# Cross attention into a silu MLP on one core: the opening reordered, softmax sums in halves, x loads moved

## The chip, the cores and the metric

The kernel runs on one core of one Trainium2 chip. The metric is the device time of one execution in microseconds (us); lower is better. Before the change the median of five runs is 222.99 us (222.26 to 225.28).

## The reference

For each of 8 batches and 8 heads there are 512 tokens `x` and 32 states `state` of width 64. Tokens read from states and states read from tokens; the results are joined along the sequence, the heads are merged, and 4352 rows of width 512 go through a two-layer MLP with silu (2048 wide).

```python
scores = scale * np.matmul(x, state.transpose(0, 1, 3, 2))
a = softmax(scores); xread = np.matmul(a, state)        # 512 rows of a batch
scores2 = scale * np.matmul(state, x.transpose(0, 1, 3, 2))
a2 = softmax(scores2); sread = np.matmul(a2, x)         # 32 rows of a batch
...
h = x @ w_in                                            # 512 -> 2048
return (h / (1 + exp(-h))) @ w_out                      # 2048 -> 512
```

## The kernel before

All products are in bf16 with fp32 sums. The kernel never builds `xread`: with `W1[b] = state[b] @ w_in` (line 248, from the transposed states `sbd`), the first MLP layer of a batch's 512 tokens is `W1[b]` times the transposed probabilities `aT`. For a batch b the names are:

- `x_f` holds x in fp32, two buffers by b % 2. `x_n` is x in bf16 (with columns of ones for the softmax sums), `x_u` the same in another order, `xT` its transpose. Batches 0 and 1 are cast by `cast_x` and transposed on PE (`x_T`, evicted by `x_Te`); batches 2 to 7 are cast by `cast_xu` and transposed by a DMA on the SP queue (`x_Td`).
- `sc` makes the scores (PE), `ex` their exponentials `en` (ACT), `norm_s` the row sums and reciprocals `rs` (DVE), `norm_m` the probabilities `an` (DVE or POOL). `a_T` (PE) or `a_Td` (a DMA on the SP queue, batches 3 to 7) transposes them to `aT`. `sread_m`, `sread_n`, `sread_t` make the 32 state rows.
- `g1(b, ft)` is one of 16 blocks of the first layer, two matmuls of 512 columns and a silu on ACT; `g2` is one matmul of the second layer, 64 to a batch. `G2(b, ft)` is four of them. The 256 state rows of all batches are batch 8.
- `w1_m` and `w1_e` compute and evict one quarter j of `W1`; `W1x` is both. Quarter j needs the load `load_wi(j)`, and `g2` of ft 4j to 4j+3 needs `load_wo(j)`. These loads are issued by POOL, one after the other, and turn fp32 into bf16 on the way.
- `warm(n, bank, w)` issues n matmuls of zeros that nobody reads.

The order of each engine's queue is written out by hand (`tc.manual_schedule`): each engine takes its instructions in program order. The program has an opening (lines 328 to 411), a hand-laid mixture of batches 0 and 1 (413 to 486), and then `phase(k, fill)` for k = 1 to 7: 64 `g2` of batch k are numbered as steps, and `fill` hangs the attention and the 16 `g1` of batch k + 1 on given steps. `att_head` places the transposing load `x_Td` and the scores of a batch, `att_tail` its softmax, `W1`, `a_Td` and `g1`.

In the opening of the kernel before, POOL issues `load_wi(0)`, `load_wo(0)`, `load_st(1)`, `load_wi(1)` as soon as the states of batch 0 are cast; only batch 0 goes through attention; x of batch 1 is loaded by POOL between weight loads, and batch 1's casts, transposes, scores and softmax lie between the `g1` and `G2` of batch 0. In phase k, `load_x(k+2)` is issued on SP at the phase's start, `cast_xu(k+2)` follows on POOL in the same phase, and `a_Td(k+1)` is issued on SP a few us later.

Of the kernel before, what the change touches and what calls it, by code (L numbers as in the profile page):

```python
# [8 lines left out]
FP32 = mybir.dt.float32  # L9
# [10 lines left out]
def kernel(  # L20
# [8 lines left out]
    nc = tc.nc  # L29
# [10 lines left out]

    zeros = pers.tile([128, 512], BF16, name="zeros")
    ident = pers.tile([128, 128], BF16, name="ident")
    st0_f = pers.tile([128, 128], FP32, name="st0_f")
    st_nat = pers.tile([128, B, 128], BF16, name="st_nat")
    sbd = pers.tile([128, B, KT, 2, NS], BF16, name="sbd")
    x_f = [pers.tile([128, KT, 2, 256], FP32, name=f"x_f{i}") for i in range(2)]
# [30 lines left out]
    def cp(eng, dst, src):  # L77
        if eng == "dve":
            nc.vector.tensor_copy(dst, src)  # L79
        elif eng == "pool":  # L80
            nc.gpsimd.tensor_copy(dst, src)  # L81
        else:
            nc.scalar.activation(dst, src, func=COPY, bias=0.0)  # L83
# [5 lines left out]
    def load_x(b, eng, kt=0, n=4):  # L89
        dst = x_f[b % 2][:, ds(kt, n)].rearrange("p k h e -> p (k h) e")  # L90
        eng.dma_start(dst, x_src(b, kt, n))  # L91
# [4 lines left out]
    def load_wi(j):  # L96
        nc.gpsimd.dma_start(
            w_in_sb[:, :, ds(512 * j, 512)], win_re[:, :, ds(512 * j, 512)]
        )

    def load_wo(j):
        nc.gpsimd.dma_start(w_out_sb[:, ds(4 * j, 4), :], wout_re[:, ds(4 * j, 4), :])

    def load_st(b):
        nc.gpsimd.dma_start(st_nat[:, b, :], state[b].rearrange("h ns d -> ns h d"))


    def cast_x(b, eng, kts=(0, 1, 2, 3)):
        for kt in kts:
            for h in range(2):  # L110
                cp(
                    eng,
                    x_n[b % 2][:, kt, :, ds(2 + D * h, D)],
                    x_f[b % 2][:, kt, h, :].rearrange("p (c d) -> p c d", c=4),
                )
# [11 lines left out]
    def x_T(b, kt, bk):  # L127
        v = bf(bk).rearrange("p (k c t) -> p k c t", k=2, c=4)
        for c in range(4):
            nc.tensor.transpose(  # L130
                v[:, kt % 2, c, :], x_n[b % 2][:, kt, c, ds(2, 128)], ident[:]
            )

    def x_Te(b, kt, n, bk, eng):
        v = bf(bk).rearrange("p (k c t) -> p k c t", k=2, c=4)
        cp(eng, xT[b % 2][:, ds(kt, n)], v[:, ds(kt % 2, n)])
# [32 lines left out]
    def ex(b, kt, n, bk):  # L169
        v = bank[bk][:].rearrange("p (k q s) -> p k q s", k=2, q=8)  # L170
        nc.scalar.activation(  # L171
            en[b % 2][:, :, :, ds(kt, n), :].rearrange("p h c k s -> p k (h c) s"),
            v[:, ds(kt % 2, n)],
            func=EXP,
            bias=0.0,
            scale=SCALE,
        )
# [83 lines left out]
    def w1_e(b, j, bks, engs):  # L261
        for half in range(2):
            cp(engs[half], W1[b % 2][:, half, ds(512 * j, 512)], bank[bks[half]][:])
# [55 lines left out]
    def warm(n, bk, w=128):  # L319
        for i in range(n):  # L320
            nc.tensor.matmul(  # L321
                bank[bk][:, 0:w], zeros[:, 0:128], zeros[:, 0:w], start=True, stop=True,
                skip_group_check=True,
            )

    with tc.manual_schedule():

        nc.scalar.dma_start(st0_f[:], state[0].rearrange("h ns d -> ns h d"))
        for kt in range(KT):
            load_x(0, nc.sync, kt, 1)  # L330
        nc.vector.memset(zeros[:], 0.0)  # L331
        nc.vector.memset(sbd[:], 0.0)
        for i in range(2):
            nc.vector.memset(x_n[i][:, :, :, 1:131:129], 1.0)
        make_identity(nc, ident[:])
        nc.scalar.preload_act_table(EXP)
        cp("pool", st_nat[:, 0, :], st0_f[:])
        load_wi(0)
        load_wo(0)
        load_st(1)  # L340
        load_wi(1)
        warm(30, "o0")

        XB = ("o0", "o1", "w0", "w1")
# [13 lines left out]
            w1_e(b, j, bks, engs)  # L358

        def exs(b):  # L360
            ex(b, 0, 2, "a0")
            ex(b, 2, 2, "a1")

        def xTs(b, q, eng):
            for kt in (2 * q, 2 * q + 1):
                x_T(b, kt, AB[q])
            x_Te(b, 2 * q, 2, AB[q], eng)

        def scs(b, q):
            for kt in (2 * q, 2 * q + 1):  # L370
# [1 line left out]


        cast_x(0, "dve", (0,))
        x_T(0, 0, XB[0])
        x_Te(0, 0, 1, XB[0], "act")
        cast_x(0, "dve", (1,))
        st_T(0, "a1", "act", "dve")
        cast_x(0, "dve", (2, 3))
        warm(8, "w1")  # L380
        x_T(0, 1, XB[1])
        x_Te(0, 1, 1, XB[1], "act")
        sc(0, 0, SB[0])
        ex(0, 0, 1, SB[0])
        warm(10, "w1")
        x_T(0, 2, XB[2])
        x_Te(0, 2, 1, XB[2], "act")
        sc(0, 1, SB[1])
        ex(0, 1, 1, SB[1])
        warm(5, "o0")  # L390
        x_T(0, 3, XB[3])
        x_Te(0, 3, 1, XB[3], "dve")
        warm(4, "o0")
        for kt in (2, 3):
            sc(0, kt, SB[kt])
            ex(0, kt, 1, SB[kt])
        norm_s(0, 0, 2)
        norm_m(0, "pool", 0, 2)
        norm_s(0, 2, 2)
        norm_m(0, "dve", 2, 2)  # L400
        nc.scalar.preload_act_table(SILU)
        warm(8, "o0", 512)
        w1_m(0, 0, ("w0", "w1"))
        w1_e(0, 0, ("w0", "w1"), ("act", "act"))
        a_T(0, (("a0", "dve"), ("a1", "dve")))
        warm(2, "o0", 512)
        load_x(1, nc.gpsimd, 0, 2)
        load_x(1, nc.gpsimd, 2, 2)
        load_wo(1)
        load_wi(2)  # L410


        for ft in range(4):
            g1(0, ft)
        G2(0, 0)
        st_T(1, "a0", "dve", "dve")
        sread_m(0, "a1")
        sread_n(0, "a1")
        G2(0, 1)
        sread_t(0, "a1", "dve")  # L420
        G2(0, 2)
        W1x(0, 1, AB, DA)
        G2(0, 3)
        g1(0, 4)
        cast_x(1, "dve", (0, 1))
        cast_x(1, "pool", (3,))
        g1(0, 5)
        W1x(1, 0, AB, DA)
        g1(0, 6)
        cast_x(1, "dve", (2,))  # L430
        load_wo(2)
        load_wi(3)
        load_wo(3)
        load_x(2, nc.gpsimd)
        for b in range(2, B):
            load_st(b)
        g1(0, 7)
        xTs(1, 0, "dve")
        xTs(1, 1, "act")
        G2(0, 4)  # L440
        scs(1, 0)
        scs(1, 1)
        exs(1)
        nc.scalar.preload_act_table(SILU)
        G2(0, 5)
        W1x(0, 2, HB, DD)
        norm_s(1)
        norm_m(1, "dve")
        G2(0, 6)
        g1(0, 8)  # L450
        G2(0, 7)
        g1(0, 9)

        W1x(1, 1, AB, ("act", "act"))
        g1(0, 10)
        G2(0, 8)
        g1(0, 11)
        a_T(1, (("a0", "dve"),))
        G2(0, 9)
        g1(1, 0)  # L460
        W1x(1, 2, AB, DA)
        G2(0, 10)
        g1(1, 1)
        W1x(0, 3, AB, DA)
        G2(0, 11)
        g1(0, 12)
        g1(0, 13)
        W1x(1, 3, AB, DA)
        cast_xu(2, "dve", (0, 1))
        cast_xu(2, "pool", (2, 3))  # L470
        x_Td(2)

        G2(0, 12)
        g1(0, 14)
        G2(0, 13)
        g1(0, 15)
        g1(1, 2)
        G2(0, 14)
        st_T(2, "a0", "dve", "dve")
        g1(1, 3)  # L480
        G2(0, 15)
        g1(1, 4)
        g1(1, 5)
        for tt in range(4):
            o_e(0, tt, OB[tt], "dve")
        load_x(3, nc.sync)


        WP = (("w0", "w1"), ("h0", "h1"))
# [22 lines left out]
        def att_head(fill, b, s0, s1):  # L512
            add(fill, s0, L(st_T, b, "a0", "dve", "dve"))
            add(fill, s0, L(x_Td, b))
            add(fill, s1, L(scs, b, 0))
            add(fill, s1 + 2, L(scs, b, 1))

        def att_tail(fill, b, s, a0, sg, dg):
            add(fill, s, L(exs, b), L(W1p, b, 0), L(norm_s, b))
            add(fill, s, L(norm_m, b, "dve", 0, 2), L(norm_m, b, "pool", 2, 2))  # L520
            add(fill, s, L(nc.scalar.preload_act_table, SILU))
            add(fill, s + 14, L(W1p, b, 1), L(sread_m, b, "a1"), L(sread_n, b, "a1"))
            if b == 2:
                add(fill, a0, L(a_T, b, (("a0", "act"),)))
            else:
                add(fill, s, L(a_Td, b))
            add(fill, a0 + 2, L(sread_t, b, "a1", "dve"))
            for i in range(16):
                add(fill, sg + dg * i, L(g1, b, i))

        fill = {}
        for i in range(6, 16):
            add(fill, i - 6, L(g1, 1, i))
        add(fill, 1, L(sread_m, 1, "a1"), L(sread_n, 1, "a1"))
        add(fill, 3, L(sread_t, 1, "a1", "dve"))
        add(fill, 3, L(cast_xu, 3))
        add(fill, 6, L(scs, 2, 0))
        add(fill, 8, L(scs, 2, 1))
        att_tail(fill, 2, 10, 33, 38, 1.55)
        att_head(fill, 3, 37, 58)  # L540
        phase(1, fill)

        for k in range(2, 7):
            fill = {}
            if k + 2 < B:
                load_x(k + 2, nc.sync)
            att_tail(fill, k + 1, 0, 24, 35, 1.8)
            if k + 2 < B:
                add(fill, 0, L(cast_xu, k + 2))
                att_head(fill, k + 2, 34, 56)  # L550
            phase(k, fill)
# [45 lines left out]
```

The softmax here doesn't subtract the row's maximum and nothing guards it: scores larger than these inputs give would overflow.

## Time and profile before

| | us |
|---|---|
| median of five runs | 222.99 (222.26 to 225.28) |
| the profiled execution, its own time | 222.26 |
| its span, first to last instruction | 220.5 |
| PE busy (with 67 warm matmuls of zeros) | 212.9 |
| ACT, DVE, POOL busy | 133.0, 83.6, 40.7 |
| TensorE clock granted | 1.000 |

Two tables of the page give the weights of the groups. A busy PE matmul of 512 columns has a duration of 379 ns, but such matmuls follow each other every 216 ns, because they overlap; sums over PE are therefore made from the starts. In the timeline a line reads: start, length, engine, line, operation, output<-input, shape and count, and in brackets how long the engine idled before it and for whom. Lines of `cp` (79, 81, 83) serve many casts and evictions, so they are told apart by their tiles.

### The profile page before, as it was taken

The page shows a single profiled execution, that of the slowest core. Times are in us where ns is not written, and L with a number is a line of the kernel's source. Part 1 is how long each engine was busy: PE and PEld are TensorE (multiplying, and loading weights), DVE is VectorE, ACT ScalarE, POOL GpSimd, SP SyncE. Part 2 cuts the span into 40 slices and gives each one's busy share as a digit, 9 for nine tenths or more (in the row PEclk, how much of TensorE's full clock was granted, in tenths as well). Part 3 has the DMA queues.
Part 4 walks back from the last instruction along what each step waited for, and adds up shares of the span by engine and source line. Part 5 has one row for each costly group of instructions (what it writes and reads, how often), then busy time and mean ns, then how long its engine had stood idle before and what let it go on. Part 6 is the DMA issues. An engine that isn't in the chain of part 4 may idle for free.

```text
span 220.5 us, 4100 instructions
## 1 busy us (share of the span) xinstructions
PE 212.9 (97%) x1659; PEld 103.6 (47%) x1659; DVE 83.6 (38%) x162; ACT 133.0 (60%) x219; POOL 40.7 (18%) x78
## 2 busy tenths in 40 slices
PE   7999999999999999999999999997999999999993
PEld 7644443443445344444444444443453444566552
DVE  4736445614910671048213831285105701111110
ACT  3755966579587927684577647781769377533210
POOL 4643822005200060005200250025000200000000
PEclk9999999999999999999999999999999999999999
DMA  6999998892251576138611763075511311111112
GB/s 199 152 246 244 171 250 132 123 292 68 95 109 37 123 210 146 48 84 230 166 48 50 218 167 92 3 231 154 95 48 48 98 48 49 50 49 48 48 51 95
DMA packets 36068, 26.52 MB, mean 120 GB/s; under 512 B 20816, under 2 KB 31312, under 8 KB 36048
## 3 DMA queue, kind: packets, MB, share of 16 engines
q1 hardware_dynamic: 28800, 19.27, 32.3%
q0 software_dynamic: 6688, 6.52, 16.5%
q10 hardware_dynamic: 560, 0.46, 0.6%
q8 instruction: 13, 0.21, 0.4%
q14 instruction: 7, 0.06, 0.1%
HBM read 17.30 MB, written 8.91 MB: 119 GB/s over the span
## 4 chain that ended last, share of the span: by engine, by line
PE 84%; DMA 8%; POOL 2%; ACT 2%; issue 2%; DVE 1%; ACTq 0%; POOLq 0%; DVEq 0%
PE ps_o L296 45%; PE ps_h L272 24%; DMA w_in_sb<-in_moe_w_in_dram 6%; PE ps_h L283 3%; PE ps_w L296 3%; DMA aT<-an 2%; PE ps_o L321 2%; PE ps_h L251 2%; PE ps_w L251 2%; PE ps_a L160 1%; POOL an L186 1%; PE ps_a L218 1%; POOL x_f L91 1%; PE ps_w L321 1%; PE ps_a L251 1%
## 5 line engine op out<-in xcount | busy, mean ns | idle before, releaser
L296 PE MATMUL ps_o<-w_out_sb,g 128*128 128x512 bf16 x480 | 129.5, 379 | 0.0
L280 ACT ACTIVATE g<-ps_h 128x512 bf16<-128x512 f32 x128 | 75.7, 597 | 53.7 <-PE ps_h L272 52.1
L272 PE MATMUL ps_h<-aT,W 128*128 128x512 bf16 x256 | 75.4, 379 | 1.9 <-DMA aT<-an 1.4
L296 PEld LDWEIGHTS <-g 128*128 128x128 bf16 x512 | 47.6, 98 | 51.7 <-issue 2.8
L79 DVE COPY o_sb<-ps_o 128x512 f32<-128x512 f32 x30 | 20.6, 688 | 89.8 <-PE ps_o L296 89.7
L272 PEld LDWEIGHTS <-W 128*128 128x128 bf16 x256 | 24.5, 98 | 32.3 <-issue 1.7
L186 POOL TENSOR_TENSOR an<-en,rs 128x512 bf16<-128x512 bf16 x7 | 10.0, 1425 | 91.7 <-ACT W L83 52.1
L81 POOL CAST x_u<-x_f 128x256 bf16<-128x256 f32 x44 | 15.6, 404 | 26.5 <-DMA x_f<-in_x_dram 24.8
L79 DVE CAST W<-ps_w 128x512 bf16<-128x512 f32 x24 | 15.3, 680 | 4.5 <-PE ps_w L251 4.5
L83 ACT ACTIVATE W<-ps_h 128x512 bf16<-128x512 f32 x24 | 13.1, 602 | 0.1
L291 ACT ACTIVATE g_s<-ps_h 128x256 bf16<-128x256 f32 x16 | 6.1, 384 | 11.1 <-PE ps_h L283 11.1
L181 DVE TENSOR_REDUCE rs<-en 128x32 f32<-128x1024 bf16 (+1 forms) x9 | 9.9, 1099 | 5.9 <-ACT en L171 5.9
L283 PE MATMUL ps_h<-xsT,w_in_sb 128*128 128x256 bf16 x64 | 9.6, 273 | 0.0
L296 PE MATMUL ps_w<-w_out_sb,g 128*128 128x512 bf16 x32 | 9.5, 379 | 0.0
L171 ACT ACT_TABLE_LOAD x7 | 9.0, 1283 | 0.1
L171 ACT ACTIVATE en<-ps_a 128x512 bf16<-128x512 f32 (+1 forms) x16 | 8.4, 568 | 0.2
L283 PEld LDWEIGHTS <-w_in_sb 128*128 128x128 bf16 x64 | 6.3, 98 | 4.1
L251 PEld LDWEIGHTS <-sbd 64*32 64x32 bf16 x256 | 3.2, 89 | 10.1 <-issue 10.0
L321 PE MATMUL ps_o<-zeros 128*128 128x128 bf16 (+1 forms) x49 | 6.7, 309 | 1.2 <-DVE zeros L331 1.2
L510 ACT ACT_TABLE_LOAD x6 | 7.7, 1283 | 0.1
L160 PEld LDWEIGHTS <-xT 128*128 128x128 bf16 x128 | 5.9, 98 | 3.5 <-DVE xT L79 0.3
L321 PEld LDWEIGHTS <-zeros 128*128 128x128 bf16 x67 | 6.0, 127 | 1.9 <-DVE zeros L331 1.2
(63 smaller groups left out, 124.9 us busy)
## 6 DMA issues: line engine op xcount, KB each, us to landing
out_dram<-o_sb SPq DMA_DIRECT2D x32, 256.0 KB, 2.4
x_f<-in_x_dram SPq DMA_DIRECT2D x5, 1024.0 KB, 6.9
w_in_sb<-in_moe_w_in_dram POOLq DMA_DIRECT2D x4, 512.0 KB, 9.4
w_out_sb<-in_moe_w_out_dram POOLq DMA_DIRECT2D x4, 512.0 KB, 9.1
x_f<-in_x_dram SPq DMA_DIRECT2D x4, 256.0 KB, 3.7
x_f<-in_x_dram POOLq DMA_DIRECT2D x2, 512.0 KB, 8.5
x_f<-in_x_dram POOLq DMA_DIRECT2D x1, 1024.0 KB, 13.5
out_dram<-o_sb ACTq DMA_DIRECT2D x1, 256.0 KB, 2.4
```

The source lines that it names most:

```text
L79: nc.vector.tensor_copy(dst, src)
L81: nc.gpsimd.tensor_copy(dst, src)
L83: nc.scalar.activation(dst, src, func=COPY, bias=0.0)
L171: nc.scalar.activation(en[b % 2][:, :, :, ds(kt, n), :].rearrange("p h c k s -> p k (h c) s"), v[:, ds(kt % 2, n)], func=EXP, bias=0.0, sc ...
L181: nc.vector.tensor_reduce(v, en[b % 2][:, :, :, ds(kt, n), :], axis=AX, op=ADD)
L186: e.tensor_tensor(an[b % 2][:, :, :, ds(kt, n), :].rearrange("p h c k s -> p (h c) k s"), en[b % 2][:, :, :, ds(kt, n), :].rearrange("p h ...
L251: nc.tensor.matmul(bank[bks[half]][ds(32 * kt, 32), :], sbd[ds(64 * half, 64), b, kt, half, :], w_in_sb[ds(64 * half, 64), kt, ds(512 * j, ...
L272: nc.tensor.matmul(bk[:], W1[b % 2][:, half, ds(128 * ft, 128)], aT[b % 2][:, half, :, :], start=(half == 0), stop=(half == 1), skip_group ...
L280: nc.scalar.activation(g[b % 2][:, ft, :], bk[:], func=SILU, bias=0.0)
L283: nc.tensor.matmul(bk[:, 0:256], w_in_sb[:, kt, ds(128 * ft, 128)], xsT[:, kt, :, :, :], start=(kt == 0), stop=(kt == KT - 1), skip_group_ ...
L296: nc.tensor.matmul(bank[bk][:, c0:c1], src[:, ft, ds(128 * tt, 128)], w_out_sb[:, ft, c0:c1], start=(ft == 0), stop=(ft == 15), skip_group ...
L321: nc.tensor.matmul(bank[bk][:, 0:w], zeros[:, 0:128], zeros[:, 0:w], start=True, stop=True, skip_group_check=True,)
```

## The change

- States of batch 1 get an fp32 buffer of their own (`st_f[1]`), loaded by SP. All of x of batch 1 is loaded by SP directly behind x of batch 0, in four pieces.
- Casts of batches 0 and 1 are split over DVE, POOL and ACT (`cast_x` takes a list of heads). `load_wi(0)` and `load_wo(0)` stand on POOL behind four casts, the last of them of batch 1's first piece; the other weight loads stand behind POOL's two products of batch 0's softmax, and the last two behind its product of batch 1's.
- Batch 1's casts, transposes, scores and exponentials are done in the opening, ahead of the first `W1x(0, 0)`; one pair of activation table loads goes. The mixture of batches 0 and 1 is laid anew: ten `g1` of batch 1 instead of six stand in it.
- `att_tail` forms the softmax sums and products of a batch in two halves, the first product on POOL, the second on DVE.
- `load_x` of batches 4 to 7 moves one phase ahead: it is issued behind `x_Td` in `att_head`, or at step 6 of phase 1 (batch 4). Phase 1 places batch 2's attention 4 steps earlier.

```diff
+        for kt in range(KT):
+            if kt == 2:
+                nc.sync.dma_start(st_f[1][:], state[1].rearrange("h ns d -> ns h d"))
+            load_x(1, nc.sync, kt, 1)
...
-        cp("pool", st_nat[:, 0, :], st0_f[:])
-        load_wi(0)
-        load_wo(0)
-        load_st(1)
-        load_wi(1)
...
+        cp("pool", st_nat[:, 0, :], st_f[0][:])
         x_T(0, 0, XB[0])
         x_Te(0, 0, 1, XB[0], "act")
         cast_x(0, "dve", (1,))
         st_T(0, "a1", "act", "dve")
-        cast_x(0, "dve", (2, 3))
+        cast_x(0, "dve", (2,), (0,))
+        cast_x(0, "pool", (2,), (1,))
+        cast_x(0, "dve", (3,), (0,))
+        cast_x(0, "pool", (3,), (1,))
+        cast_x(1, "pool", (0,), (1,))
+        load_wi(0)
+        load_wo(0)
...
         x_T(0, 3, XB[3])
+        cast_x(1, "dve", (0,), (0,))
         x_Te(0, 3, 1, XB[3], "dve")
...
+        cast_x(1, "dve", (1,))
+        cast_x(1, "act", (2,))
         norm_s(0, 0, 2)
         norm_m(0, "pool", 0, 2)
+        x_T(1, 0, "o0")
+        x_T(1, 1, "o0")
+        x_Te(1, 0, 2, "o0", "dve")
+        cp("act", st_nat[:, 1, :], st_f[1][:])
+        cast_x(1, "act", (3,))
+        warm(8, "a0")
+        st_T(1, "a1", "dve", "dve")
         norm_s(0, 2, 2)
-        norm_m(0, "dve", 2, 2)
+        norm_m(0, "pool", 2, 2)
+        x_T(1, 2, "o1")
+        x_T(1, 3, "o1")
+        x_Te(1, 2, 2, "o1", "act")
+        warm(4, "a0")
+        sc(1, 0, "w0")
+        sc(1, 1, "w0")
+        ex(1, 0, 2, "w0")
+        warm(8, "a0")
+        sc(1, 2, "w1")
+        sc(1, 3, "w1")
+        ex(1, 2, 2, "w1")
         nc.scalar.preload_act_table(SILU)
-        warm(8, "o0", 512)
-        w1_m(0, 0, ("w0", "w1"))
-        w1_e(0, 0, ("w0", "w1"), ("act", "act"))
+        warm(8, "a0")
         a_T(0, (("a0", "dve"), ("a1", "dve")))
-        warm(2, "o0", 512)
-        load_x(1, nc.gpsimd, 0, 2)
-        load_x(1, nc.gpsimd, 2, 2)
+        W1x(0, 0, ("o0", "o1"), DA)
+        load_wi(1)
         load_wo(1)
         load_wi(2)
+        load_wo(2)
+        norm_s(1, 0, 2)
+        norm_m(1, "pool", 0, 2)
+        norm_s(1, 2, 2)
+        norm_m(1, "dve", 2, 2)
+        warm(6, "o0")
...
+        for j in (1, 2, 3):
+            n = 3 * j - 3
+            g1(0, 4 * j)
+            g1(1, n)
+            W1x(1, j, AB, DA)
...
         def att_head(fill, b, s0, s1):
             add(fill, s0, L(st_T, b, "a0", "dve", "dve"))
             add(fill, s0, L(x_Td, b))
+            if 4 < b + 1 < B:
+                add(fill, s0, L(load_x, b + 1, nc.sync))
...
         def att_tail(fill, b, s, a0, sg, dg):
-            add(fill, s, L(exs, b), L(W1p, b, 0), L(norm_s, b))
-            add(fill, s, L(norm_m, b, "dve", 0, 2), L(norm_m, b, "pool", 2, 2))
+            add(fill, s, L(exs, b), L(W1p, b, 0))
+            add(fill, s, L(norm_s, b, 0, 2), L(norm_m, b, "pool", 0, 2))
+            add(fill, s, L(norm_s, b, 2, 2), L(norm_m, b, "dve", 2, 2))
...
-        for i in range(6, 16):
-            add(fill, i - 6, L(g1, 1, i))
-        add(fill, 1, L(sread_m, 1, "a1"), L(sread_n, 1, "a1"))
-        add(fill, 3, L(sread_t, 1, "a1", "dve"))
-        add(fill, 3, L(cast_xu, 3))
-        add(fill, 6, L(scs, 2, 0))
-        add(fill, 8, L(scs, 2, 1))
-        att_tail(fill, 2, 10, 33, 38, 1.55)
+        for i in range(10, 16):
+            add(fill, i - 10, L(g1, 1, i))
+        add(fill, 2, L(scs, 2, 0))
+        add(fill, 3, L(scs, 2, 1))
+        att_tail(fill, 2, 6, 30, 35, 1.8)
+        add(fill, 6, L(cast_xu, 3), L(load_x, 4, nc.sync))
...
-            if k + 2 < B:
-                load_x(k + 2, nc.sync)
```

More of the change, by code (lines that the diff above doesn't have):

```diff
@@ L42 @@
     ident = pers.tile([128, 128], BF16, name="ident")
-    st0_f = pers.tile([128, 128], FP32, name="st0_f")
+    st_f = [pers.tile([128, 128], FP32, name=f"st_f{i}") for i in range(2)]
     st_nat = pers.tile([128, B, 128], BF16, name="st_nat")
@@ L105, in load_st, with cast_x @@
         nc.gpsimd.dma_start(st_nat[:, b, :], state[b].rearrange("h ns d -> ns h d"))
-    def cast_x(b, eng, kts=(0, 1, 2, 3)):
+    def cast_x(b, eng, kts=(0, 1, 2, 3), hs=(0, 1)):
         for kt in kts:
-            for h in range(2):
+            for h in hs:
                 cp(
@@ L326 @@
     with tc.manual_schedule():
-        nc.scalar.dma_start(st0_f[:], state[0].rearrange("h ns d -> ns h d"))
+        nc.scalar.dma_start(st_f[0][:], state[0].rearrange("h ns d -> ns h d"))
         for kt in range(KT):
             load_x(0, nc.sync, kt, 1)
+        for kt in range(KT):
+            if kt == 2:
+                nc.sync.dma_start(st_f[1][:], state[1].rearrange("h ns d -> ns h d"))
+            load_x(1, nc.sync, kt, 1)
         nc.vector.memset(zeros[:], 0.0)
@@ L360, in exs @@
         def exs(b):
[L361 to L367, printed above, removed]
+            for q in range(2):
+                ex(b, 2 * q, 2, AB[q])
         def scs(b, q):
@@ L384 @@
         ex(0, 0, 1, SB[0])
-        warm(10, "w1")
+        warm(8, "w1")
         x_T(0, 2, XB[2])
@@ L389 @@
         ex(0, 1, 1, SB[1])
-        warm(5, "o0")
+        warm(3, "w1")
         x_T(0, 3, XB[3])
+        cast_x(1, "dve", (0,), (0,))
         x_Te(0, 3, 1, XB[3], "dve")
-        warm(4, "o0")
+        warm(3, "o0")
         for kt in (2, 3):
@@ L396 @@
             ex(0, kt, 1, SB[kt])
+        cast_x(1, "dve", (1,))
+        cast_x(1, "act", (2,))
         norm_s(0, 0, 2)
         norm_m(0, "pool", 0, 2)
-        norm_s(0, 2, 2)
-        norm_m(0, "dve", 2, 2)
+        x_T(1, 0, "o0")
[5 more added lines that the diff above has]
+        st_T(1, "a1", "dve", "dve")
+        norm_s(0, 2, 2)
+        norm_m(0, "pool", 2, 2)
[10 more added lines that the diff above has]
+        ex(1, 2, 2, "w1")
         nc.scalar.preload_act_table(SILU)
-        warm(8, "o0", 512)
-        w1_m(0, 0, ("w0", "w1"))
-        w1_e(0, 0, ("w0", "w1"), ("act", "act"))
+        warm(8, "a0")
         a_T(0, (("a0", "dve"), ("a1", "dve")))
-        warm(2, "o0", 512)
-        load_x(1, nc.gpsimd, 0, 2)
-        load_x(1, nc.gpsimd, 2, 2)
+        W1x(0, 0, ("o0", "o1"), DA)
+        load_wi(1)
         load_wo(1)
         load_wi(2)
[L413 to L430, printed above, removed]
-        load_wo(2)
+        load_wo(2)
+        norm_s(1, 0, 2)
[3 more added lines that the diff above has]
+        warm(6, "o0")
+        g1(0, 0)
+        g1(0, 1)
+        sread_m(0, "a0")
+        sread_n(0, "a0")
+        g1(0, 2)
+        g1(0, 3)
         load_wi(3)
@@ L436 @@
             load_st(b)
[L437 to L457, printed above, removed]
-        a_T(1, (("a0", "dve"),))
[L459 to L483, printed above, removed]
+        G2(0, 0)
+        sread_t(0, "a0", "dve")
+        sread_m(1, "a1")
+        sread_n(1, "a1")
+        G2(0, 1)
+        sread_t(1, "a1", "dve")
+        a_T(1, (("a0", "dve"),))
+        G2(0, 2)
+        W1x(0, 1, AB, DA)
+        G2(0, 3)
+        W1x(1, 0, AB, DA)
+        for j in (1, 2, 3):
[3 more added lines that the diff above has]
+            W1x(1, j, AB, DA)
+            g1(0, 4 * j + 1)
+            g1(0, 4 * j + 2)
+            G2(0, 4 * j)
+            g1(0, 4 * j + 3)
+            G2(0, 4 * j + 1)
+            g1(1, n + 1)
+            if j == 3:
+                cast_xu(2, "dve", (0, 1))
+                cast_xu(2, "pool", (2, 3))
+                x_Td(2)
+                st_T(2, "a0", "dve", "dve")
+            G2(0, 4 * j + 2)
+            if j < 3:
+                W1x(0, j + 1, AB, DA)
+            g1(1, n + 2)
+            G2(0, 4 * j + 3)
         for tt in range(4):
@@ L486 @@
         load_x(3, nc.sync)
+        g1(1, 9)
         WP = (("w0", "w1"), ("h0", "h1"))
```

## The prediction

> **What bounds the kernel.** I read the chain of waits first, then the timeline of the opening, the waits inside it, the stretches of 1 us for the DMA, and last the lengths of the phases.
>
> ```profile
> PE 84%; DMA 8%; POOL 2%; ACT 2%; issue 2%; DVE 1%; ACTq 0%; POOLq 0%; DVEq 0%
> ```
>
> PE carries 84% of the chain. So time can come from three places: work that leaves PE's queue, stalls of PE, and the opening before PE's stream starts. The opening and the work of batch 1, from the timeline:
>
> ```profile
> 8.26 0.83 ACT L171 ACTIVATE en<-ps_a 128x256 bf16<-128x256 f32 x2
> 9.11 1.28 ACT L401 ACT_TABLE_LOAD   x1
> 9.36 1.05 POOL L186 TENSOR_TENSOR an<-en,rs 128x512 bf16<-128x512 bf16 x1 [1.88 <-DVE rs L182]
> 10.80 1.09 ACT L83 ACTIVATE W<-ps_w 128x512 bf16<-128x512 f32 x2 [0.41 <-PE ps_w L251]
> 12.01 1.14 PE L272 MATMUL ps_h<-aT,W 128*128 128x512 bf16 x4
> ...
> 21.06 1.29 PE L130 MATMUL ps_a<-ident,x_n 128*128 128x128 bf16 x16
> 23.20 0.68 PE L160 MATMUL ps_a<-sbd,xT 128*128 128x64 bf16 x16
> ...
> 26.74 0.39 PE L272 MATMUL ps_h<-aT,W 128*128 128x512 bf16 x1 [0.21 <-DVE W L79]
> ```
>
> The first real `g1` starts at 12.01. Batch 1's 16 transposes and 16 score matmuls sit inside the paid stream at 21 to 24. Phase 2 begins at 72.73 (its first `w1_m`). Between 12.01 and 72.73 I count PE's work by starts: 224 matmuls of 512 columns at 0.2165 = 48.50; seven single `W1x` at 0.44 (a `g1` ends at 32.33, the next one starts at 32.78); batch 2's two `W1` pairs 0.96 + 1.02 (the second with its `sread_m`); scores of batches 2 and 3 at 0.46 each; two `a_T` 0.90; two more `sread_m` 0.92; 16 transposes 1.28 (21.06 to 22.34); batch 1's scores 0.51; six small transposes at 0.06. Sum 58.45, elapsed 60.72: 2.27 of stalls.
>
> The phases start at 72.73, 95.71, 118.86, 142.00, 166.67. One is 24.67 long where its neighbour takes 23.14, so 1.53 is lost there. The timeline names it, around the transposing DMA of `an`:
>
> ```profile
> 146.51 1.50 POOL L186 TENSOR_TENSOR an<-en,rs 128x512 bf16<-128x512 bf16 x1 [16.76 <-ACT W L83]
> 148.04 1.23 SPq L208 DMA_TRANSPOSE aT<-an  x1
> 152.94 0.60 PE L272 MATMUL ps_h<-aT,W 128*128 128x512 bf16 x2 [1.35 <-DMA aT<-an]
> ```
>
> That DMA landed after 4.9 us where the median of the five is 3.1. The phase before it issued at 124.89, so it landed about 128.0, for a `g1` at 128.28: a margin of 0.3 us everywhere, lost once in this execution.
>
> Last, the stretches of the DMA (PE, PEld, DVE, ACT, POOL busy; clock; DMA share; GB/s):
>
> ```profile
> 4.00:5.00 1.00, 1.00 (x12) 1.00 (x10) 0.50 (x3) 0.00 (x0) 1.00 (x2) 1.00 1.09 350
> 8.00:9.00 1.00, 0.84 (x13) 0.48 (x12) 0.97 (x3) 0.83 (x3) 0.00 (x0) 1.00 1.24 204
> ```
>
> Plain x moves at 350 GB/s (1.05 MB in 3.0 us). Weight quarters, counted as written, move at about 200; the waits put three landings at 24.8, 28.6 and 31.1, so some 3.1 us each.
>
> **Opening, moved: +3.35.** In the kernel before, `load_wi(0)` was issued at 4.32 and landed 5.5 later, 9.8. x of batch 0 is through at 5.6; x of batch 1 behind it at 350 GB/s puts its first piece at 7.0 and its last at 9.4 (0.6 for receipt, as the second piece of batch 0 shows: 0.59 MB moved by 4.05, cast at 4.73). POOL waits for the first piece, casts it (0.40) and issues `load_wi(0)` at 7.4, which by the old 5.5 lands at 12.9, and `load_wo(0)` 3.3 later. That is covered by ACT, whose queue is now the long one: from 8.85 to 9.1 the exponentials of batch 0 end; two casts 0.75, the state cast 0.26, two casts 0.75 (priced by ACT's 0.38 for 256 columns): 10.85. Transposes on PE 0.45, `x_Te` 1.02: 12.35. Two exponentials 1.09 with their wait: 13.6. Table 1.28: 14.9. Half of `W1` 0.60: about 15.4. DVE and POOL arrive with it: sums of the first half end at 9.85, `x_Te` 10.55, two state copies 11.15, sums of the second half 12.1, POOL's product 1.05 to 1.46, `a_T` 0.6, its two evictions 0.75, W1's other half 0.69: 15.3. So `g1(0, 0)` starts at 15.36 instead of 12.01. Bounds: 14.6 if the casts overlap as paired exponentials do (0.83 for two waits no piece), 18.5 under the slow transfer below. I take 15.36, since every term has a row.
>
> Weights behind it: `load_wi(1)` leaves POOL after its second product, about 13.4, and lands near 19; `W1x(0, 1)` is wanted near 21. Each further pair feeds 16 `g2`, seven `g1` and two `W1x` (3.46 + 3.03 + 0.88 = 7.4 us of PE) and moves in 6.2. They cost nothing; if POOL's products were late by 3 us, they would cost the excess over 2. SP takes five more issues (0.47 to 0.72 each) before 6, with nothing due on it until `x_Td(2)` at 39 or later; POOL loses three (0.70 to 0.94).
>
> The Trainium skill, "DMA: Bandwidth & Descriptors" (Issuing engines are not separate DMA queues), says that transfers issued from different engines share the same 16 DMA engines. This case agrees (shares over 1.0 in nearly every stretch from 7 to 33 us), and it speaks against putting 1 MB of x ahead. By the rule the weights pay those 3 us, which the sum above has from the rows; without it `load_wi(0)` would land near 10 and the opening still end with ACT.
>
> **Work that leaves the stream: -1.85.** 1.28 + 0.51 + 0.06 of batch 1 now lie where PE waited anyway, among warm matmuls.
>
> **Stalls of the mixture: 2.27 becomes 0.8.** Those that go: the wait for `W1x(0, 2)`, whose eviction stood behind batch 1's exponentials (26.14, 26.74); the bank wait behind `a_T(2)` at 59.38, now seven steps ahead of `st_T(3)` instead of four. Those that stay: the first four `g1`, paced by two banks and 0.60 of silu (0.6), and `g1(1, 0)` one `g1` behind its `W1x` (0.2). Bounds 0.3 and 1.8: the low end has the pace alone in part, the high one adds a late `xT(2)`, whose first DMA took 5.6 and now has about 6 us before `scs(2, 0)` at step 2. I take 0.8. So -1.47.
>
> **Phases: -1.53.** Sums in halves let POOL begin after one reduction of 0.68 and a reciprocal of 0.25 instead of 1.22 and 0.35, and after one exponential instead of two: `an` is ready 0.6 to 1.1 earlier. x no longer moves while `a_Td` does. The margin of 0.3 grows to 0.9 or more. Behind it: `x_Td` shares its time with `load_x`, but it has 10 us to `scs` and took 4.3; outputs on SP queue behind both, with four buffers. I take the whole 1.53; bounds 0 and 1.53.
>
> The Trainium skill, "SBUF — State Buffer" (Who interferes with whom), states that a DVE instruction with two SBUF inputs contends with a POOL instruction that reads SBUF. The rows agree: POOL's product took 1.05 beside sums and 1.50 beside DVE's product. By the rule alone, with both products locked in turn, the later one ends no earlier than before, the phases gain 0 and the sum would be 222.5. By the rows they now start 0.9 apart and most of POOL's product is past.
>
> Sum: 222.26 (profiled execution: span 220.5 and 1.76 around it) + 3.35 - 1.85 - 1.47 - 1.53 = 220.76. The median lies 0.73 above that execution; I add 0.2 for what of that spread the change leaves: **221.0**.
>
> **Rivals.**
> - *Slower: the opening is bound by x.* The page's first slice has only 199 GB/s. At that rate x of both batches and the states (2.23 MB) need 11.2 us from 2.0, the last piece lands at 13.2, ACT's cast of it ends at 13.95 instead of 10.85, and all behind it moves by 3.1: 224.1, up to 227 with `load_wi(0)` late as well. It decides from a first `g1` later than 16.9. Against it: 350 GB/s as soon as x flows. For it: the new third stream of state rows and POOL's loads among them.
> - *The stall stays.* If the late landing at 152.9 has nothing to do with x or `an`, 1.53 remains: 222.5. For it: one in five, at no special place.
> - *The opening overlaps better.* Start 14.7, stalls 0.3: 219.8 with the 0.2.
> - *The clock falls in the sparse opening.* The first zeros follow each other every 0.107 us until about 5.5, later 0.056: half rate for 4.3 us. Once more, in paid work, costs 2.15: 223.1. Against it: some 4 of 6.3 us stay busy with 34 warm matmuls and transposes.
>
> **Chances.** Forecast 0.42 (220.0 to 222.0), slow x 0.22 (half of it above 225.2), stall stays 0.14, better overlap 0.16, clock 0.06. Faster by over 1% means below 220.76, slower above 225.2; this is about what a measurement tells from no change. Faster: 0.16 and half of 0.42, 0.37. Slower: 0.11 and a little of the clock, 0.13. Same: 0.50. The range 219.5 to 224.9 leaves out the lowest 0.06 and the highest 0.13.
>
> **What would show it.** The first `g1` near 15.4 with the eviction of `W1` behind a table load; no transposes of x after it; phase 2 near 72.8; phases 2 to 5 all 23.1; `a_Td` issued 5.0 to 5.5 after the phase's first `w1_m` instead of 6.0. I am wrong if the first `g1` waits for a DMA, if a weight quarter is waited for, or if the stall reappears.

## The result and the profile after

| | before | after |
|---|---|---|
| median of all runs (lowest to highest) | 222.52 (221.45 to 226.09, 95 runs) | 221.76 (221.06 to 222.99, 53 runs) |
| profiled execution: own time, span | 222.26, 220.5 | 221.61, 219.8 |

The ratio after to before is 0.996, with a 95% interval of 0.995 to 0.997. The change gains some 0.8 us, which is real and is less than 1%. The five runs shown before the prediction had a median of 222.99; with 95 runs it is 222.52.

The chain of waits of the kernel after (its shares by engine) shows less of the DMA and more of PE:

```profile
PE 91%; DMA 2%; SPq 2%; ACT 1%; DVE 1%; POOL 0%; issue 0%
```

The DMA had 8% of the chain before. Next the timeline of the kernel after, the end of its opening and then the first `w1_m` of phases 2 to 6:

```profile
9.52 0.72 ACT L83 ACTIVATE x_n<-x_f 128x256 bf16<-128x256 f32 x2 [0.23 <-DMA x_f<-in_x_dram]
...
13.68 1.28 ACT L423 ACT_TABLE_LOAD   x1
14.24 0.41 PE L251 MATMUL ps_o<-w_in_sb,sbd 64*32 64x512 bf16 x8
14.80 0.68 DVE L79 CAST W<-ps_o 128x512 bf16<-128x512 f32 x1
14.97 0.60 ACT L83 ACTIVATE W<-ps_o 128x512 bf16<-128x512 f32 x1
15.53 0.49 PE L321 MATMUL ps_o<-zeros 128*128 128x128 bf16 x6 [0.88 <-DVE W L79]
15.86 1.03 PE L272 MATMUL ps_h<-aT,W 128*128 128x512 bf16 x4
...
73.31 0.41 PE L251 MATMUL ps_w<-w_in_sb,sbd 64*32 64x512 bf16 x8
...
96.46 0.41 PE L251 MATMUL ps_w<-w_in_sb,sbd 64*32 64x512 bf16 x8
...
165.90 0.41 PE L251 MATMUL ps_w<-w_in_sb,sbd 64*32 64x512 bf16 x8
```

The opening ends at 15.86 instead of 12.01. The second half of the eviction of `W1` stands behind a table load, as said; but then six warm matmuls into bank `o0`, which holds `W1`'s first half, wait for DVE (15.53) and put 0.29 between the end of the evictions (15.57) and the first `g1`. The phases begin at 73.31, 96.46, 119.60, 142.75 and 165.90, each 23.14 or 23.15 long (two of these starts are not printed above). The long one, 24.67, is gone. Around the first transpose of `an` the timeline reads:

```profile
76.73 1.06 POOL L186 TENSOR_TENSOR an<-en,rs 128x512 bf16<-128x512 bf16 x1 [18.15 <-DVE rs L182]
77.43 0.91 DVE L186 TENSOR_TENSOR an<-en,rs 128x512 bf16<-128x512 bf16 x1
78.48 1.23 SPq L208 DMA_TRANSPOSE aT<-an  x1
...
80.56 0.34 SPq L317 DMA_DIRECT2D out_dram<-o_sb  x1
```

The transpose is issued 5.17 after the phase's first `w1_m` (78.48 less 73.31), not 6.04 as before (148.04 less 142.00). The `g1` that needs it now starts 0.75 to 1.24 after the landing, where the margin before was 0.26 to 0.39. All five land after 3.0 to 3.1, as the view of their tile says in its last line:

```profile
DMA to landing us min/median/max: 3.0/3.0/3.1
```

Where the time went, between the two profiled executions (their spans are printed to 0.1, so the fourth and fifth rows are rough):

| stretch | before | after | difference | prediction |
|---|---|---|---|---|
| start to the first `g1` | 12.01 | 15.86 | +3.85 | +3.35 |
| first `g1` to phase 2 | 60.72 | 57.45 | -3.27 | -3.32 |
| four phases, 2 to 5 | 93.94 | 92.59 | -1.35 | -1.53 |
| the rest of the span | 53.83 | 53.90 | +0.07 | 0 |
| around the span | 1.76 | 1.81 | +0.05 | 0 |
| own time | 222.26 | 221.61 | -0.65 | -1.50 |

### The profile page after: what moved, and what is told of

It is laid out like the page before. It is cut to its first block, busy times and chain, and to the rows that moved or that the text cites. A ratio compares the mean times of both kernels' runs of the same rounds, so it can differ in the third digit from the quotient of the medians.

```text
span 219.8 us, 4155 instructions
## 1 busy us (share of the span) xinstructions
PE 212.5 (97%) x1678; PEld 105.1 (48%) x1678; DVE 83.8 (38%) x171; ACT 131.4 (60%) x221; POOL 40.7 (18%) x78
## 4 chain that ended last, share of the span: by engine, by line
PE 91%; DMA 2%; SPq 2%; ACT 1%; DVE 1%; POOL 0%; issue 0%
PE ps_o L296 50%; PE ps_h L272 25%; PE ps_w L296 4%; PE ps_h L283 3%; DMA x_f<-in_x_dram 2%; PE ps_w L251 2%; PE ps_h L251 2%; PE ps_a L218 1%; SPq L91 1%; PE ps_a L160 1%; PE ps_a L251 1%; ACT x_n L83 1%; PE ps_a L202 1%; DVE W L79 1%; POOL an L186 0%; ACT xT L83 0%
## 5 line engine op out<-in xcount | busy, mean ns | idle before, releaser
L81 POOL CAST x_u<-x_f 128x256 bf16<-128x256 f32 x44 | 17.8, 452 | 4.4 <-DMA x_f<-in_x_dram 4.4
L181 DVE TENSOR_REDUCE rs<-en 128x16 f32<-128x512 bf16 x16 | 10.5, 658 | 3.2 <-ACT en L171 3.2
L79 DVE CAST W<-ps_a 128x512 bf16<-128x512 f32 x7 | 4.8, 692 | 14.2 <-PE ps_a L251 14.2
L321 PEld LDWEIGHTS <-zeros 128*128 128x128 bf16 x86 | 7.2, 124 | 2.3 <-DVE zeros L335 1.2
L83 ACT ACTIVATE W<-ps_a 128x512 bf16<-128x512 f32 x7 | 4.2, 598 | 5.4 <-PE ps_a L251 5.4
```

What stands on the lines that cost most here:

```text
L181: nc.vector.tensor_reduce(v, en[b % 2][:, :, :, ds(kt, n), :], axis=AX, op=ADD)
```

## The experiments

The theory at first was the prediction's own: the new opening costs more than the two starts in it save, and the lost phase went because `an` is ready earlier and x moves elsewhere. The rivals were that x alone does it, and that the late landing has a third cause. All times below are medians; each ratio is to the kernel before on the same chip, in the same rounds.

**The old opening with the new phases.** The kernel before, with the halves of sums and products and with the early `load_x`:

```diff
             add(fill, s0, L(x_Td, b))
+            if 4 < b + 1 < B:
+                add(fill, s0, L(load_x, b + 1, nc.sync))
...
-            add(fill, s, L(exs, b), L(W1p, b, 0), L(norm_s, b))
-            add(fill, s, L(norm_m, b, "dve", 0, 2), L(norm_m, b, "pool", 2, 2))
+            add(fill, s, L(exs, b), L(W1p, b, 0))
+            add(fill, s, L(norm_s, b, 0, 2), L(norm_m, b, "pool", 0, 2))
+            add(fill, s, L(norm_s, b, 2, 2), L(norm_m, b, "dve", 2, 2))
...
-        add(fill, 3, L(cast_xu, 3))
+        add(fill, 3, L(cast_xu, 3), L(load_x, 4, nc.sync))
...
-            if k + 2 < B:
-                load_x(k + 2, nc.sync)
```

> The opening and the mixture of batches 0 and 1 as before the change; softmax sums in halves and x one phase ahead as after it. Theory A (the opening and mixture cost 0.6 us net, phase 2 starting at 73.31 instead of 72.73, and the phases give 1.3 to 1.5): phase 2 starts at 72.7 to 73.0, phases 2 to 6 are all 23.1 to 23.2 long, and the time is 1.1 to 1.5 us below the kernel before, so 0.4 to 0.7 us below the changed kernel. Theory B (the gain comes from batch 1's work leaving the stream, the lost 1.53 us in one phase was chance): within 0.3 us of the kernel before.

Measured: 220.65 (220.29 to 223.68, 12 runs), ratio 0.9926, interval 0.9895 to 0.9956. Its timeline has the first `g1` and phase 2 at:

```profile
11.76 1.14 PE L272 MATMUL ps_h<-aT,W 128*128 128x512 bf16 x4
...
72.26 0.41 PE L251 MATMUL ps_w<-w_in_sb,sbd 64*32 64x512 bf16 x8
```

Phase 2 starts 1.05 earlier than in the kernel after, and no phase is longer than 23.15. So the part of the change that lies in the opening costs: without it the kernel is faster, by 0.8 us if the two ratios are compared (0.34% of 222.5) and by 1.1 if the medians are. The two intervals still overlap by a little (this one ends at 0.9956, the other begins at 0.995); a second kernel with the old opening, below, gives 0.9928 again. This is the lowest median of the study.

**The new opening with the old phases.** The reverse: the kernel after, with whole sums and `load_x` at the start of each phase (the lines above undone).

> The reverse: the new opening and mixture, sums in one piece and x loaded at each phase's start as before the change. Theory A: 0.4 to 0.8 us slower than the kernel before, one or more phases longer than 23.3 with a g1 that waits for the transposing DMA of an. Theory B: as fast as the changed kernel, 0.6 to 0.9 us below the kernel before.

Measured: 223.54 (223.00 to 224.25, 12 runs), ratio 1.0035, interval 1.0018 to 1.0052: slower than before. Two transposes landed late, and PE waited for both:

```profile
84.55 0.60 PE L272 MATMUL ps_h<-aT,W 128*128 128x512 bf16 x2 [1.40 <-DMA aT<-an]
...
154.53 0.61 PE L272 MATMUL ps_h<-aT,W 128*128 128x512 bf16 x2 [0.37 <-DMA aT<-an]
```

**One of the two parts in the phases alone.** Two kernels made from the kernel after. The first takes the sums and products whole again and leaves the early `load_x`:

```diff
-            add(fill, s, L(exs, b), L(W1p, b, 0))
-            add(fill, s, L(norm_s, b, 0, 2), L(norm_m, b, "pool", 0, 2))
-            add(fill, s, L(norm_s, b, 2, 2), L(norm_m, b, "dve", 2, 2))
+            add(fill, s, L(exs, b), L(W1p, b, 0), L(norm_s, b))
+            add(fill, s, L(norm_m, b, "dve", 0, 2), L(norm_m, b, "pool", 2, 2))
```

> The changed kernel with the sums in one piece again; x stays one phase ahead. Theory H (the halves make an ready earlier and so remove the wait for its transpose): an's transpose is issued 5.9 to 6.1 us after a phase's first w1_m, a phase is longer than 23.3, and the time is 0.5 to 1.3 us above the changed kernel. Theory X (x out of the way of the transpose is what removes it): transposes land after 3.0 to 3.2 us in all phases, all phases 23.15, time within 0.3 us of the changed kernel.

The second leaves the halves and loads x late again:

```diff
-            if 4 < b + 1 < B:
-                add(fill, s0, L(load_x, b + 1, nc.sync))
...
-        add(fill, 6, L(cast_xu, 3), L(load_x, 4, nc.sync))
+        add(fill, 6, L(cast_xu, 3))
...
+            if k + 2 < B:
+                load_x(k + 2, nc.sync)
```

> The changed kernel with x loaded at each phase's start as before the change; sums stay in halves. Theory H: an's transpose is issued 5.0 to 5.6 us after a phase's first w1_m, and although it may land after up to 4.9 us it is waited for by at most 0.5 us; time within 0.3 us of the changed kernel. Theory X: a transpose lands after 4 us or more, at least one phase is longer than 23.5, and the time is 0.5 to 1.3 us above the changed kernel.

Measured: whole sums 223.08 (222.70 to 223.61, 12 runs), ratio 1.0014, interval 0.9996 to 1.0033; late x 222.01 (221.07 to 223.08, 12 runs), ratio 0.9968, interval 0.9947 to 0.9989. So in these kernels the halves are worth about 1.2 us (0.54% between the ratios 1.0014 and 0.996), and the place of `load_x` 0.2, which lies inside the intervals. With late x the transposes take up to 4.3, yet only one cost PE anything:

```profile
152.60 0.60 PE L272 MATMUL ps_h<-aT,W 128*128 128x512 bf16 x2 [0.36 <-DMA aT<-an]
```

With whole sums and x out of the way a transpose was still late by 1.7 (4.75 instead of 3.05), in phase 2 this time. Its timeline:

```profile
79.62 1.23 SPq L208 DMA_TRANSPOSE aT<-an  x1
80.94 2.39 SPq L317 DMA_DIRECT2D out_dram<-o_sb  x2
...
84.41 0.60 PE L272 MATMUL ps_h<-aT,W 128*128 128x512 bf16 x2 [1.24 <-DMA aT<-an]
```

No packet of x was moving then, so x is not what made this one late. The DMA view of that kernel for 82 to 83 us (queue, kind: packets, MB, share of 16 engines) has a second queue:

```profile
q1 hardware_dynamic: 224, 0.26, 80.1%
q8 instruction: 1, 0.02, 5.5%
```

One packet of instructions of 16,384 B, 2.59 after the issue. There are 13 of them in an execution to some 3,365 recorded PE instructions (matmuls and weight loads): one to 259 on average, with distances from 168 to 360. We take them for PE's instruction fetches. The Trainium skill, "Runtime: NRT & Kernel Launch" (Instruction fetch mechanics), says that a sequencer refills its instructions in blocks of 16 KiB, 256 instructions, through a DMA queue of its own; the size here agrees, and the distance does on average. The page calls the cost mostly hidden, and whether it was hidden from a transpose was tested next.

**The fetch moved, the sums left whole.** 16 more warm matmuls in the opening shift every later fetch in the stream; nothing else differs from the kernel with whole sums.

```diff
+        warm(16, "w0")
         warm(6, "o0")
```

> The changed kernel with the sums in one piece, as in the run that was 1.3 us slower, and 16 more warm matmuls in bank w0 where PE waits for the first eviction of W1 (0.9 us). Theory F (the transposing DMA lands late when a 16 KB instruction fetch falls 1.1 to 2.9 us behind its issue; the fetches are PE's, one in some 256 of its instructions, so 32 more PE instructions move them some 3 us forward): the fetch at 82.2 moves to about 79, all five transposes land after 3.0 to 3.2 us, all phases are 23.1 to 23.2, and the time is 0.9 to 1.4 us below that run though the sums are as late as there. Theory M (sums in one piece are too late by themselves, fetch or no fetch): the first of the five transposes is waited for by over 1 us as before, and the time stays.

Measured: 221.55 (221.18 to 222.37, 12 runs), ratio 0.9957, interval 0.9935 to 0.9980. This is 1.3 us below the kernel with whole sums by the ratios (0.57%), for 16 matmuls more. The tile `aT` and, below it, the DMA of 78.9 to 80.3 us show why:

```profile
L208 SPq DMA_TRANSPOSE aT<-an x5: 1232/1233/1337, 79.5 to 172.1; - x5
...
DMA to landing us min/median/max: 3.0/3.0/3.1
```

```profile
q8 instruction: 1, 0.02, 5.7%
```

The fetch went from 82.21 to 79.10, ahead of the transpose at 79.47. The transpose is issued as late as before (79.47 less 73.43 is 6.04), and all five now land in time; the phases are 23.15 each. The fetch is the cause of that late landing, shown by moving the fetches and nothing else in the phases (one profiled execution and 12 runs of each kernel, on two chips, so that the times compare by their ratios alone). With the fetches moved, whole sums are as fast as the halves (0.9957 and 0.996): what the halves are worth depends on where the fetches fall.

Over 12 profiles there are 60 of these transposes. Seven landed after 3.87 us or more, and every one had a fetch that began 1.06 to 2.89 after its issue; the one of the kernel before, at 148.04, had it 2.74 after. The next in length, 3.82, had no fetch; it is in the kernel with late x, and packets of x were moving until 2.4 after its issue, and the same transpose of the kernel after landed after 3.04: x alone can hold one up, here by 0.8. A fetch begun up to 0.5 after the issue left 3.0 to 3.5. With sums in halves, seven fetches at 2.48 to 2.75 did no harm (3.0 to 3.2; one at 1.53 did, 4.3), while with whole sums all four at 2.59 to 2.89 did.

The packets in the traces show a difference between these two groups. A transpose moves as 1,024 packets of 256 B, and undisturbed the last of them ends 2.6 after the issue. The output transfer behind it is issued 1.3 after the transpose with whole sums (80.94 less 79.62) and 2.1 with halves, and its packets of 2,048 B begin 2.4 and 2.9 after the transpose's issue. In the four late landings 5 to 12 of the 1,024 packets ended later than 2.7; in six of the seven harmless cases all had ended by 2.6, in the seventh (late x) by 2.8. So a fetch at that distance did harm only where output packets had begun before the transpose was through. That both are needed is not shown: no run moved the output alone.

**The opening: the bank of the warm matmuls.** The kernel after, with the six warm matmuls in another bank:

```diff
-        warm(6, "o0")
+        warm(6, "w0")
```

> The changed kernel; the six warm matmuls ahead of the first g1 write bank w0 instead of o0. Theory W (those six wait for the evictions of the first quarter of W1 out of o0, and so put 0.33 us between the eviction and the first g1): the first g1 starts at 15.5 instead of 15.86 and the time falls by 0.2 to 0.4 us. Rival: the first g1 waits for the eviction anyway and the second batch of waits eats it; within 0.1 us of the changed kernel.

Measured: 221.31 (220.83 to 221.87, 8 runs), ratio 0.9935, interval 0.9908 to 0.9962. The first `g1` follows the evictions directly:

```profile
15.41 1.04 PE L272 MATMUL ps_h<-aT,W 128*128 128x512 bf16 x4 [0.44 <-DVE W L79]
```

It starts 0.45 earlier and phase 2 begins at 72.99, 0.32 earlier. Of the 0.45 some 0.12 is not the bank's: DVE's eviction began at 14.68 in this execution, not at 14.80. It beats the kernel after by 0.25% in the ratios, with overlapping intervals.

**The opening: the queues ahead of it.** In addition the second product of batch 0 on DVE, and the state rows of batch 1 loaded on ACT's queue, ahead of x:

```diff
+        nc.scalar.dma_start(st_f[1][:], state[1].rearrange("h ns d -> ns h d"))
...
-            if kt == 2:
-                nc.sync.dma_start(st_f[1][:], state[1].rearrange("h ns d -> ns h d"))
...
-        norm_m(0, "pool", 2, 2)
+        norm_m(0, "dve", 2, 2)
...
-        warm(6, "o0")
+        warm(6, "w0")
```

> As the run with the warm matmuls in bank w0, and batch 0's second softmax product on DVE as before the change, and the states of batch 1 loaded from ACT's queue instead of between the x pieces on SP's. If the opening's start passes to the end one to one: third x piece cast on ACT from 9.3 instead of 9.52, a_T at 13.2 to 13.4 instead of 13.69, first g1 at 15.2 to 15.4, time 0.4 to 0.7 us below the changed kernel. If ACT's table load sets the start alone: first g1 not before 15.5, no more gain than the run with the warm matmuls moved.

Measured: 221.42 (221.06 to 221.81, 12 runs), ratio 0.9939, interval 0.9914 to 0.9964: nothing more than the bank alone. `a_T` came earlier (13.27 instead of 13.69), and the timeline shows two other things behind it:

```profile
13.58 1.28 ACT L422 ACT_TABLE_LOAD   x1
...
14.16 0.41 PE L251 MATMUL ps_o<-w_in_sb,sbd 64*32 64x512 bf16 x8 [0.29 <-DMA w_in_sb<-in_moe_w_in_dram]
...
15.38 1.04 PE L272 MATMUL ps_h<-aT,W 128*128 128x512 bf16 x4 [0.37 <-DVE W L79]
```

The first weight quarter and ACT's queue with its table load end within 0.7 of one another (14.16 and 14.86). Neither POOL's product nor the states' rows set the end, and the weight is no longer covered.

**Two waits of the old opening.** The first experiment's kernel, with `W1x(0, 2)` one `G2` later, so that its eviction has more time, and the `a_T` of batch 2 two steps earlier:

```diff
         G2(0, 5)
+        G2(0, 6)
         W1x(0, 2, HB, DD)
...
-        G2(0, 6)
-        g1(0, 8)
         G2(0, 7)
+        g1(0, 8)
...
-        att_tail(fill, 2, 10, 33, 38, 1.55)
+        att_tail(fill, 2, 10, 31, 38, 1.55)
```

> The old opening with the new phases, and two waits taken out of it: W1x(0, 2) one G2 later, so that it no longer meets the landing of its weights, and batch 2's a_T two steps earlier, so that the bank is evicted before the transpose of batch 3's states. Expected 0.5 to 0.8 us below the old opening with the new phases alone, phase 2 at 71.5 to 71.8. Rival: the mixture is bound by the arrival of the weights (quarters land at 24.8, 28.6, 31.1); then a later G2 waits for w_out and at most 0.5 us is left.

Measured: 220.85 (219.87 to 222.14, 12 runs), ratio 0.9928, interval 0.9901 to 0.9954: as the first experiment, and not faster as expected. The first `g1` to phase 2 took 60.43 there and 60.50 in the first. The wait came back at another place, for the same DVE:

```profile
12.21 0.41 PE L251 MATMUL ps_w<-w_in_sb,sbd 64*32 64x512 bf16 x8 [1.70 <-DMA w_in_sb<-in_moe_w_in_dram]
...
28.89 0.82 PE L272 MATMUL ps_h<-aT,W 128*128 128x512 bf16 x3 [0.21 <-DVE W L79]
```

The first of the two lines was not looked for: in this execution the first weight quarter landed 7.9 us after its issue, where it took 5.5 in the profile of before.

**The kernel before, profiled once more**, unchanged, for the spread of its runs (221.45 to 226.09).

> The kernel before, profiled a second time. Its runs lie between 221.5 and 226.1 where the changed kernel's lie between 221.1 and 223.0. Theory J (the first weight quarter lands 5.5 to 8 us after its issue, and where it is late the old opening waits for it): the first g1 starts between 11.8 and 14, and the time less 222.26 is that start less 12.0 plus the waits for an's transpose less 1.5. Theory F says for those waits: a late landing only where a 16 KB instruction fetch falls 1 to 3 us behind an issue.

Measured: 223.57, span 221.8, which is 1.31 above the first profiled execution. Its timeline:

```profile
11.44 0.41 PE L251 MATMUL ps_w<-w_in_sb,sbd 64*32 64x512 bf16 x8 [0.79 <-DMA w_in_sb<-in_moe_w_in_dram]
...
106.52 0.61 PE L272 MATMUL ps_h<-aT,W 128*128 128x512 bf16 x2 [0.73 <-DMA aT<-an]
...
154.24 0.60 PE L272 MATMUL ps_h<-aT,W 128*128 128x512 bf16 x2 [1.26 <-DMA aT<-an]
```

The first quarter landed after 7.1, and put the first `g1` at 12.69: +0.68. Two transposes landed after 4.2 and 4.8, each with a fetch behind it (1.39 and 2.74 after the issue): the four phases +0.81. The stretch between is 0.19 shorter. The three make 1.30 of the 1.31. The same program has one or two late transposes, and a landing of the first weight that varies.

**The first weight quarter alone.** The first experiment's kernel, with the next weight loads issued only after the products of batch 0, so that nothing is queued behind `load_wi(0)`:

```diff
         load_wi(0)
-        load_wo(0)
-        load_st(1)
-        load_wi(1)
...
         warm(2, "o0", 512)
+        load_wo(0)
+        load_st(1)
+        load_wi(1)
```

> The old opening with the new phases; w_out's first quarter, batch 1's states and w_in's second quarter are issued behind batch 0's softmax product on POOL instead of directly behind w_in's first quarter. If the transfers queued behind the first quarter are what delays its landing in some executions: it lands 5.5 us or less after its issue, the first g1 starts by 12.0, and the times of the runs lie within 1 us of each other; but w_out's first quarter lands near 16 and the second w_in near 19, so the G2 and W1x that need them wait and the time is 0.5 to 2.5 us above the old opening with the new phases. If they are not: the spread stays.

Measured: 224.37 (223.63 to 225.64, 4 runs), ratio 1.0101, interval 1.0054 to 1.0149. The first quarter landed after 8.0, alone:

```profile
12.47 0.44 PE L251 MATMUL ps_w<-w_in_sb,sbd 64*32 64x512 bf16 x8 [2.09 <-DMA w_in_sb<-in_moe_w_in_dram]
```

The transfers queued behind it are not what delays it in this execution. Of the 16 packets of 4 B that end the transfer 14 were moved by 5.1 after the issue, one at 5.9 and the last at 7.7 (in the kernel before all by 5.2): it is a straggler that is late, not the whole load. Over the 12 profiles the landing took 5.5, 5.6, 7.1, 7.9 and 8.0 with the old opening, and 5.5 to 5.8 in all seven with the new one, where the load is issued some 4 us later; what makes it vary stays open.

The time is 3.7 above the first experiment's kernel, more than expected, and part of that is the clock. After the wait of 2.09 the granted clock was 0.50 from 12.73 on for 3.4 us, in which the first six matmuls of `g1` took 2.34 (the first four took 1.14 in the first experiment); in the run with two waits taken out, PE waited 1.70 at the same place and the granted clock stayed at 1.00. Two of the four runs were granted 0.985 and 0.989 on average, the others 0.990 and 1.000; the first two are those above 225, so the spread of 2 us says nothing certain about the landing.

## Why the prediction was right, and where it was off

The forecast of 221.0 is 0.76 below the median of 221.76, inside the range and with the sign and size called likeliest: a gain of less than 1%. The sum for the profiled execution was 220.76 against 221.61.

- *Opening, +3.35.* It was +3.85: the mis-sized term, and 0.50 of the 0.85 that the sum missed. Its terms came late one after the other: the third piece of batch 1's x was cast on ACT at 9.52 instead of 9.1, and the evictions ended at 15.57, where the sum had 15.36. The rest, 0.29, is the warm matmuls ahead of the first `g1`. They were counted as filler that costs nothing, but they write into a bank that was still being read; the step to check was which bank each of them names. In the experiment with the other bank the first `g1` came 0.45 earlier, some 0.33 of it by the bank.
- *`load_wi(0)` covered by ACT.* Only just. It was issued at 8.27, not 7.4, since POOL waited for pieces of x, and landed 5.8 later, at 14.0, not 12.9; `W1`'s matmuls began at 14.24. That left 0.2, and the faster opening ran into it. The 5.5 held in all seven executions with the new opening (up to 5.8), but with the old one it was 7.1 to 8.0 in three of five: one profile was little to rest a cover on.
- *Work that leaves the stream and the stalls of the mixture, -1.85 and -1.47.* They were -3.27 together, against -3.32; the stalls left over are 0.85 if the work is taken as counted.
- *Phases, -1.53.* Near in time (-1.35), wrong in cause. The long phase lost 1.52; but the first phase is 23.15 after and was 22.98, which gives back 0.17. The prediction said that a larger margin would cover a late landing. By its own rows it could not cover it whole: PE had waited 1.35, and `an` was to be ready 0.6 to 1.1 earlier. In the kernel after, no transpose landed late, so the margin was not drawn on. In the phase that had lost 1.5 the fetch now began 0.14 ahead of the transpose, as the new opening has more PE instructions (3,365 recorded, before 3,325): for that one the forecast was lucky. In phase 2 a fetch began 2.65 behind the transpose, where with whole sums one at 2.59 made it land after 4.75; with the halves it landed after 3.02. In the first experiment, with the old opening, the fetch stayed 2.55 behind the transpose of the phase that had lost 1.5, and that one landed after 3.04. So the halves kept the landing itself on time, which the prediction had no term for. The other half of its reason, x out of the way, was worth no more than the intervals leave open. What made the landing late was the instruction fetch.
- *The two products and their contention.* By the rows of the phases POOL's product took 1.06 instead of 1.46 to 1.51, DVE's 0.87 to 0.91 instead of 0.69. They start 0.7 apart (76.73 and 77.43), not 0.9. So DVE's, which starts second, paid 0.2 and POOL's won 0.4. By the rule alone the transposes would have been issued no earlier; they were issued 0.87 earlier (6.04 less 5.17).
- *The rivals.* Slow x was present in small: pieces came 0.4 late, not 3.1. "The stall stays" had part of its premise right, since the cause was neither x nor `an` but the fetch; yet with an earlier `an` a fetch at nearly the same distance did no harm, so it was not independent of `an`. The opening did not overlap better. No clock was lost: the mean is 0.997, but the granted clock was below 1.00 only from 218.57 on, in the last 1.3 us of the span.
- *The median.* 0.2 was added for what spread is left; it was 0.15. The median of before lies 0.26 above its profiled execution, not 0.73 as the five runs had it.

## What to carry to other kernels

When one of several equal steps is late without a reason in its own neighbours, look at the instruction queue of the DMA as well. Here a fetch came to some 259 PE instructions of a long unrolled stream, and 16 matmuls more far ahead moved it off one step; in the same way any change moves it onto others. A step that is on time in one profile may be so by where the fetches fell, so compare several kernels before a part of a change is given the credit. A change of several parts is tried in its parts: here the part in the phases is worth more alone than with the opening. Filler in an opening is free only if its banks, too, are free.

## What the runs showed of the hardware

- An instruction fetch of one 16,384 B packet can hold up an SBUF to SBUF transpose: all seven landings of 3.87 us or more, instead of 3.0 to 3.1, had one 1.06 to 2.89 after the issue (the next, 3.82, had packets of x beside it and no fetch). With the fetch moved ahead of the transpose all five landed after 3.0 to 3.1. Seven fetches at 2.48 to 2.75 did no harm where the output's packets began 2.9 after the transpose's issue and not 2.4.
- The first casting weight load landed after 5.5 to 8.0 us in the profiled executions, 8.0 of them with nothing queued behind it.
- After PE had waited 2.09 us in the opening the granted clock was 0.50 for 3.4 us; after a wait of 1.70 in another kernel it stayed at 1.00.
- 16 matmuls more made a kernel 1.3 us faster (ratio 1.0014 to 0.9957).
